# Second layer of the first MLP by seven products: plain products ahead of the sums, long-lived activations in a tile of their own

## The chip, the cores and the metric

One core of a Trainium2 chip runs the whole program. The metric is the device time of one execution in microseconds (us). The kernel before took 576.33 us, the median of 3 runs (575.95 to 576.69).

## The reference, cut to what matters

```python
attn = _attn_ref(q, k, v, lam)                     # blockwise linear attention with decay, 2 x 8 x 768 x 64
x = attn.transpose(0, 2, 1, 3).reshape(1536, 512)
h = np.maximum(x @ moe_w_in, 0.0)                  # 512 -> 2048
x = (h * h @ moe_w_out)                            # 2048 -> 512
h = x @ moe2_w_in                                  # the second MLP: 512 -> 2048 -> 512
out = np.maximum(0.01 * h, h) @ moe2_w_out
```

All inputs of the MLPs but x are 64-bit floats; the output is float32.

## The kernel before, in words

Retention runs first. Then come two MLPs over 1536 tokens, held as three token tiles of 512 (t = 0, 1, 2). The 2048 hidden features are cut into four slices of 512, so each MLP has four stages, named (layer, slice): (0,0) to (0,3) and (1,0) to (1,3). In a stage, `first` computes hidden features (four groups m = 0 to 3 of 128 features for each token tile) and `second` multiplies the activated features by the slice of the second weight and adds the result to a partial sum in DRAM (`spill`).

Every float32 value is kept as a high and a low part (`split`: ScalarE copies the high part, VectorE subtracts to get the low part). A product of two matrices is three matmuls: high by high, high by low, low by high. Each matmul here has 512 columns. The weights arrive as 64-bit words and are converted on VectorE and ScalarE (`converting`), in steps laced between the matmul groups.

The change lies in stages (0,1) and (0,2), the set `seven`. There the second layer for token tiles 0 and 1 is done by `second_pair` with seven block products in place of eight (a Winograd scheme). Its operands are the weight blocks A11 to A22, sums of weight blocks S1 to S4, the activation blocks B11 (token tile 0, even m), B21 (tile 0, odd m), B22 (tile 1, odd m), and sums of activations T1 to T4. `four_sums` (lines 430 to 435) forms T1 to T4 in place in the activations r that `activate_for_seven` keeps in the dictionary `later`. T1 is split at once into the blocks of `g[1]` that no other block uses. T2 is split at once into a tile `tt[2]` of 8 KB per partition. T3 and T4 are split later (`late_split`) into the place of T1 and B21, once these have been read for the last time.

A product is computed for p = 0 and p = 1, six matmuls each. Its result stands in a PSUM bank named by `where`: "A", "B", "C", "D", one for each p. `keep` copies the bank to a buffer f on ScalarE, and a DMA adds f to DRAM. Some products are accumulated on a bank that holds an earlier one, by `start=False`: A12 B21 on A11 B11 (bank A), S4 B22 on S1 T1 (bank C), S3 T3 on S2 T2 (bank B). So bank A is copied once when it holds P1 = A11 B11, and again when it holds the sum.

What sets the order: TensorE's instructions stand in the order in which the code is written (a manual schedule for that engine). On ScalarE and VectorE a scheduler orders them at build time by priority; `tc.high_priority(offset=400)` moves the sums and splits ahead. All engines run their instructions in that order, and the waits between engines follow from the data: a matmul that adds to a bank waits for the copy that reads it. The buffers f come from a pool of nine (`fp`), which `plain()` hands out for activations and copies alike.

Of the kernel before, what the change touches and what calls it, by code (L numbers as in the profile page):

```python
# [9 lines left out]
F32 = mybir.dt.float32  # L10
F32R = mybir.dt.float32r
# [4 lines left out]
P = 128  # L16
# [3 lines left out]
def tile_retention_then_two_mlps(  # L20
# [19 lines left out]
    TT = 512  # L40
# [17 lines left out]
    def bank():  # L58
        return psum.tile([P, 512], F32, tag="ps", name="ps")

    def plain():
        return fp.tile([P, TT], F32, tag="f", name="f")

    def dma(dst, src):
        return nc.sync.dma_start(dst, src)

    def split(hi, lo, src):
        nc.scalar.copy(hi, src)
        nc.vector.tensor_tensor(out=lo, in0=src, in1=hi, op=ALU.subtract)
# [333 lines left out]
    late = ctx.enter_context(tc.tile_pool(name="late", bufs=1, reuse_waits="tile"))  # L403
# [3 lines left out]
    g, x0f, x1f, tt = {}, {}, {}, {}  # L407
# [22 lines left out]
    def four_sums(a, b, c, d):  # L430
        ve = nc.vector
        ve.tensor_tensor(out=a, in0=b, in1=a, op=ALU.subtract)
        ve.tensor_tensor(out=b, in0=c, in1=b, op=ALU.subtract)
        ve.tensor_tensor(out=c, in0=c, in1=a, op=ALU.subtract)
        ve.tensor_tensor(out=d, in0=d, in1=c, op=ALU.subtract)
# [24 lines left out]
    later = {}  # L460


    def activate_for_seven(t, m, src):
        r = plain()
        later[t, m] = r
        nc.scalar.activation(r, src, AF.Relu)
        ghi, glo = g[t]
        if (t, m % 2) != (1, 0):
            nc.scalar.square(ghi[:, m], r)
        nc.scalar.square(r, r)  # L470
        if (t, m % 2) != (1, 0):
            nc.vector.tensor_tensor(out=glo[:, m], in0=r, in1=ghi[:, m], op=ALU.subtract)
        if (t, m % 2) == (1, 1):
            h = m // 2
            with tc.high_priority(offset=400):
                four_sums(later[0, m - 1], later[1, m - 1], later[1, m], later[0, m])
                split(ghi[:, m - 1], glo[:, m - 1], later[0, m - 1])
                if h == 0:
                    tt[2] = late.tile([P, 2, 2, TT], F32R, tag="t4", name="t4")
                split(tt[2][:, 0, h], tt[2][:, 1, h], later[1, m])  # L480

    def three(ps, ops, start, stop, again=False):
        for n, (a, b) in enumerate(ops):
            nc.tensor.matmul(ps, a, b, start=start and n == 0, stop=stop and n == len(ops) - 1, skip_group_check=again)  # L484
# [103 lines left out]
    def keep(src, dst, first):  # L588
        f = plain()
        nc.scalar.copy(f, src)  # L590
        if first:
            dma(dst, f)
        else:
            nc.gpsimd.dma_start(dst, f, accum_op=ALU.add)  # L594
# [3 lines left out]
    def second_pair(s):  # L598
        begun = (0, s - 1) in seven
        (g0h, g0l), (g1h, g1l) = g[0], g[1]  # L600
        x = {
            "B11": [(g0h[:, 2 * h], g0l[:, 2 * h]) for h in range(2)],
            "B21": [(g0h[:, 2 * h + 1], g0l[:, 2 * h + 1]) for h in range(2)],
            "B22": [(g1h[:, 2 * h + 1], g1l[:, 2 * h + 1]) for h in range(2)],
            "T1": [(g1h[:, 2 * h], g1l[:, 2 * h]) for h in range(2)],
            "T2": [(tt[2][:, 0, h], tt[2][:, 1, h]) for h in range(2)],
        }
        ps = {}

        def product(p, where, a, b, start=True):  # L610
            if start:
                ps[p, where] = bank()
            ops = []
            for h in range(2):
                if a[0] == "A":
                    i, j = int(a[1]) - 1, int(a[2]) - 1
                    hi, lo = (w[:, j, (2 * p + i) * P:(2 * p + i + 1) * P] for w in wts[0, s, 1, h])
                else:
                    hi, lo = (sums[0, s, 1, h][:, part, int(a[1]) - 1, p] for part in range(2))
                bh, bl = x[b][h]  # L620
                ops += [(hi, bh), (hi, bl), (lo, bh)]
            three(ps[p, where], ops, start, True, not start)
            return ps[p, where]

        def kept(p, i, k):
            return spill[0][k][2 * p + i]

        def late_split(n, old, m):
            x[n] = x[old]
            with tc.high_priority(offset=400):  # L630
                for h in range(2):
                    split(*x[n][h], later[m(h)])

        both = range(2)
        for p in both:
            keep(product(p, "A", "A11", "B11"), partial[p]["P1"], not begun)
            yield True
        for p in both:
            keep(product(p, "C", "S1", "T1"), kept(p, 1, 1), False)
            yield True  # L640
        late_split("T3", "T1", lambda h: (1, 2 * h))
        for p in both:
            keep(product(p, "A", "A12", "B21", False), kept(p, 0, 0), False)
            yield True
        late_split("T4", "B21", lambda h: (0, 2 * h + 1))
        for p in both:
            keep(product(p, "C", "S4", "B22", False), kept(p, 0, 1), False)
            yield True
        for p in both:
            keep(product(p, "B", "S2", "T2"), partial[p]["P6"], not begun)  # L650
            yield True
        for p in both:
            keep(product(p, "D", "A22", "T4"), kept(p, 1, 0), False)
            yield True
        yield from first(0, s, 2)
        for p in both:
            keep(product(p, "B", "S3", "T3", False), partial[p]["P67"], not begun)
            yield True
        opened.add(("sums", 0, s + 1))
        if (0, s + 1) not in seven:  # L660
            for p in both:
                p1, p6, p67 = (partial[p][n] for n in ("P1", "P6", "P67"))
                for dst, src in ((p67, p1), (kept(p, 0, 1), p1), (kept(p, 0, 1), p6), (kept(p, 1, 0), p67),
                                 (kept(p, 1, 1), p67)):
                    nc.gpsimd.dma_start(dst, src, accum_op=ALU.add, max_dma_last_dim=TT)
# [97 lines left out]
```

## Time and profile before

| | us |
|---|---|
| median of 3 runs | 576.33 |
| the profiled execution, its own time | 577.08 |
| its span, first to last instruction | 575.3 |
| TensorE matmuls busy | 564.5 (98% of the span) |
| VectorE busy | 418.8 (73%) |
| ScalarE busy | 305.4 (53%) |

Matmuls overlap, so that a matmul of 0.39 us is followed by the next one 0.227 us after its start; a busy share of TensorE says only that a matmul was under way. Where TensorE waits in the MLPs is told by the list of its waits, and by the gaps in its timeline. The mean granted clock of TensorE in this execution is 0.999 of full speed.

### The profile page before, as it was taken

To read this page: it belongs to the slowest core of one execution; us is meant where nothing else is said; L and a number is where in the kernel's file an instruction comes from. 1 tells how busy PE (TensorE), PEld (TensorE's weight loads), DVE (VectorE), ACT (ScalarE), POOL (GpSimd) and SP (SyncE) were. 2 spreads that over 40 slices of the span, in tenths; PEclk is the share of its full clock that TensorE was granted. 3 is DMA by queue.
4 is the path that set the end of the run, shared out by engine and by line. 5 is a ranking of instruction groups with operands and counts; after the bars stand their busy time and mean duration, and the time that the engine had idled before them with its cause. 6 is when DMAs were issued, how large, how long until landed. Compare 5 with 4: busy or idle time off the path is not lost.

```text
span 575.3 us, 8057 instructions
## 1 busy us (share of the span) xinstructions
PE 564.5 (98%) x3075; PEld 470.5 (82%) x3075; DVE 418.8 (73%) x589; ACT 305.4 (53%) x477; POOL 84.6 (15%) x101
## 2 busy tenths in 40 slices
PE   7999999999999999999999999999999999999997
PEld 6879888888888887888888888888888888888886
DVE  3789999978618999488789999929873896217222
ACT  2344598547757587756648374543562375225110
POOL 3426000000030205346000000000203011210000
PEclk9999999999999999999999999999999999999999
DMA  8998433663193729999903216452539523661432
GB/s 174 248 203 187 157 117 129 244 197 144 40 181 113 143 74 185 188 226 181 296 25 96 77 46 220 127 166 74 97 59 247 109 27 48 74 91 56 163 111 91
DMA packets 74070, 78.12 MB, mean 136 GB/s; under 512 B 40104, under 2 KB 46512, under 8 KB 74032
## 3 DMA queue, kind: packets, MB, share of 16 engines
q1 hardware_dynamic: 60448, 60.57, 34.6%
q0 software_dynamic: 13056, 16.78, 21.0%
q8 instruction: 24, 0.39, 0.3%
q10 hardware_dynamic: 528, 0.26, 0.2%
q14 instruction: 14, 0.11, 0.1%
HBM read 52.43 MB, written 27.80 MB: 139 GB/s over the span
## 4 chain that ended last, share of the span: by engine, by line
PE 86%; DVE 7%; DMA 4%; issue 2%; ACT 1%; SPq 0%; ACTq 0%; DVEq 0%
PE ps L484 80%; DMA raw<-in_moe_w_in 3%; PE ps L296 1%; PE ps L347 1%; PE ps L279 1%; PE ps L345 1%; DMA DTr<-tab 1%; PE ps L320 1%; ACT hb L109 1%; DVE hb L113 1%; DVE rb L117 1%; DVE Pm L301 1%; DVE hb L110 0%; DVE rb L116 0%; DVE hb L120 0%
## 5 line engine op out<-in xcount | busy, mean ns | idle before, releaser
L484 PE MATMUL ps<-xhi,w1h 128*128 128x512 f32 x288 | 112.3, 390 | 0.0
L484 PE MATMUL ps<-xlo,w1h 128*128 128x512 f32 x288 | 112.2, 389 | 0.0
L484 PE MATMUL ps<-xhi,w1l 128*128 128x512 f32 x288 | 112.1, 389 | 0.0
L594 POOL DMA_DIRECT2D spill<-f x48 | 47.1, 1045 | 345.3 <-ACT f L590 345.2
L590 ACT COPY f<-ps 128x512 f32<-128x512 f32 x84 | 48.9, 585 | 74.1 <-PE ps L484 72.8
L484 PEld LDWEIGHTS ps<-xhi,w1h 128*128 128x128 f32 x288 | 54.1, 188 | 11.4 <-issue 0.2
L484 PEld LDWEIGHTS ps<-xhi,w1l 128*128 128x128 f32 x288 | 54.1, 188 | 11.2
L484 PEld LDWEIGHTS ps<-xlo,w1h 128*128 128x128 f32 x288 | 54.1, 188 | 11.2
L458 DVE TENSOR_TENSOR g0l<-f,g0h 128x512 fp32r<-128x512 f32 x52 | 35.1, 688 | 31.5 <-ACT f L454 20.0
L484 PE MATMUL ps<-w2l,g0h 128*128 128x512 f32 (+1 forms) x132 | 50.5, 383 | 0.0
L484 PE MATMUL ps<-w2h,g0l 128*128 128x512 f32 (+1 forms) x132 | 50.5, 383 | 0.0
L484 PE MATMUL ps<-w2h,g0h 128*128 128x512 f32 (+1 forms) x132 | 50.5, 383 | 0.0
L132 DVE TENSOR_TENSOR w2l<-hb,w2h 128x1024 fp32r<-128x1024 f32 x16 | 19.6, 1225 | 39.5 <-ACT w2h L130 39.2
L109 ACT ACTIVATE hb<-raw 128x1024 f32<-128x1024 f32 x32 | 36.9, 1152 | 20.2 <-DMA raw<-in_moe_w_in 9.3
L484 PE MATMUL ps<-g0l,w2h 128*128 128x512 f32 x104 | 40.5, 390 | 0.0
L484 PE MATMUL ps<-g0h,w2l 128*128 128x512 f32 x104 | 40.5, 389 | 0.0
L484 PE MATMUL ps<-g0h,w2h 128*128 128x512 f32 x104 | 40.5, 389 | 0.0
L117 DVE SCALAR_TENSOR_TENSOR rb<-raw,rb 128x1024 f32<-128x1024 uint32 x32 | 39.1, 1222 | 0.5
L120 DVE TENSOR_TENSOR hb<-hb,rb 128x1024 f32<-128x1024 f32 x32 | 39.1, 1222 | 0.4
L113 DVE SCALAR_TENSOR_TENSOR hb<-raw,hb 128x1024 uint32<-128x1024 uint32 x32 | 39.1, 1221 | 0.3
L548 DVE TENSOR_TENSOR f<-ps,f 128x512 f32<-128x512 f32 x40 | 26.3, 687 | 9.9 <-PE ps L484 9.9
L695 DVE TENSOR_TENSOR f<-ps,f 128x512 f32<-128x512 f32 (+1 forms) x25 | 16.7, 668 | 20.2 <-PE ps L484 20.2
(140 smaller groups left out, 1141.3 us busy)
## 6 DMA issues: line engine op xcount, KB each, us to landing
raw<-in_moe_w_in SPq DMA_DIRECT2D x16, 1024.0 KB, 5.6
raw<-in_moe_w_out SPq DMA_DIRECT2D x16, 1024.0 KB, 4.9
spill<-f POOLq DMA_DIRECT2D x48, 256.0 KB, 4.9
spill<-f SPq DMA_DIRECT2D x24, 256.0 KB, 2.5
f<-spill SPq DMA_DIRECT2D x24, 256.0 KB, 3.0
k<-in_k SPq DMA_DIRECT2D x12, 256.0 KB, 4.6
q<-in_q SPq DMA_DIRECT2D x12, 256.0 KB, 4.8
v<-in_v SPq DMA_DIRECT2D x12, 256.0 KB, 5.1
```

The costliest lines, as they stand in the source:

```text
L109: nc.scalar.activation(hf, w_hi.bitcast(F32), AF.Abs)
L113: yield ve.scalar_tensor_tensor(out=hb, in0=w_hi, scalar=0xC0000000, in1=hb, op0=ALU.bitwise_and, op1=ALU.bitwise_or)
L117: yield ve.scalar_tensor_tensor(out=rf, in0=w_lo, scalar=2.0 ** -52, in1=rf, op0=ALU.mult, op1=ALU.mult)
L120: yield ve.tensor_tensor(out=hf, in0=hf, in1=rf, op=ALU.add)
L132: yield ve.tensor_tensor(out=lo, in0=hf, in1=hi, op=ALU.subtract)
L279: nc.tensor.transpose(ps[:, p, :], src[:, 2 * p:2 * p + 2, :].rearrange("s h d -> s (h d)"), ident)
L458: nc.vector.tensor_tensor(out=glo, in0=r, in1=ghi, op=ALU.subtract)
L484: nc.tensor.matmul(ps, a, b, start=start and n == 0, stop=stop and n == len(ops) - 1, skip_group_check=again)
L548: ve.tensor_tensor(out=out, in0=ps[h, where], in1=other, op=ALU.add)
L590: nc.scalar.copy(f, src)
L594: nc.gpsimd.dma_start(dst, f, accum_op=ALU.add)
L695: nc.vector.tensor_tensor(out=a, in0=ps, in1=a, op=ALU.add)
```

## The change

Three edits, all for the stages (0,1) and (0,2).

1. Four of the eight activations of a stage, (t, m) = (0,1), (0,3), (1,0), (1,2), go into a tile `long` (tag "t4", 8 KB per partition, the place that `tt[2]` had) and no longer into buffers of the pool `fp`.
2. T2 has no tile of its own: it is split late, into the blocks of B11, after A11 B11 has been computed.
3. `second_pair` computes A12 B21 second and S1 T1 third. Before, it was the other way round. The splits of T2, T4 and T3 now stand behind A11 B11, A12 B21 and S1 T1.

```diff
     def activate_for_seven(t, m, src):
-        r = plain()
+        if (t, m) == (0, 0):
+            later["long"] = late.tile([P, 4, TT], F32, tag="t4", name="long")
+        r = plain() if m % 2 == t else later["long"][:, 2 * t + m // 2]
         later[t, m] = r
...
                 split(ghi[:, m - 1], glo[:, m - 1], later[0, m - 1])
-                if h == 0:
-                    tt[2] = late.tile([P, 2, 2, TT], F32R, tag="t4", name="t4")
-                split(tt[2][:, 0, h], tt[2][:, 1, h], later[1, m])
...
-            "T2": [(tt[2][:, 0, h], tt[2][:, 1, h]) for h in range(2)],
...
         for p in both:
             keep(product(p, "A", "A11", "B11"), partial[p]["P1"], not begun)
             yield True
+        late_split("T2", "B11", lambda h: (1, 2 * h + 1))
+        for p in both:
+            keep(product(p, "A", "A12", "B21", False), kept(p, 0, 0), False)
+            yield True
+        late_split("T4", "B21", lambda h: (0, 2 * h + 1))
         for p in both:
             keep(product(p, "C", "S1", "T1"), kept(p, 1, 1), False)
             yield True
         late_split("T3", "T1", lambda h: (1, 2 * h))
-        for p in both:
-            keep(product(p, "A", "A12", "B21", False), kept(p, 0, 0), False)
-            yield True
-        late_split("T4", "B21", lambda h: (0, 2 * h + 1))
         for p in both:
             keep(product(p, "C", "S4", "B22", False), kept(p, 0, 1), False)
             yield True
```

The rows below are TensorE's order in stage (0,2), where `second_pair` begins: the end of A11 B11 for p = 1, and what follows. The number behind `ps` tells the PSUM tiles apart. Before, A11 B11 stands in ps_2267 (p = 0) and ps_2278 (p = 1):

```order
L484 MATMUL ps_2267<-g0h_2069,w2l_2101 128x512
L484 MATMUL ps_2278<-g0h_2069,w2h_1714 128x512
L484 MATMUL ps_2278<-g0l_2070,w2h_1714 128x512
L484 MATMUL ps_2278<-g0h_2069,w2l_1715 128x512
L484 MATMUL ps_2278<-g0h_2069,w2h_2100 128x512
L484 MATMUL ps_2278<-g0l_2070,w2h_2100 128x512
L484 MATMUL ps_2278<-g0h_2069,w2l_2101 128x512
L484 MATMUL ps_2289<-g1h_2119,sw_1994 128x512
```

After, A11 B11 stands in ps_2255 and ps_2266 (line 483 is line 484 of before):

```order
L483 MATMUL ps_2255<-g0h_2065,w2l_2098 128x512
L483 MATMUL ps_2266<-g0h_2065,w2h_1708 128x512
L483 MATMUL ps_2266<-g0l_2066,w2h_1708 128x512
L483 MATMUL ps_2266<-g0h_2065,w2l_1709 128x512
L483 MATMUL ps_2266<-g0h_2065,w2h_2097 128x512
L483 MATMUL ps_2266<-g0l_2066,w2h_2097 128x512
L483 MATMUL ps_2266<-g0h_2065,w2l_2098 128x512
L483 MATMUL ps_2255<-g0h_2065,w2h_1708 128x512
```

Before, a bank of its own (ps_2289) follows on A11 B11, and ps_2267 comes up again twelve matmuls later; after, the matmul that follows adds to ps_2255, six matmuls after the last one that wrote to it.

ScalarE's order at the same place, before; L590 is the copy in `keep`, L466 to L470 are the activations, L68 is a split, L109 begins the conversion of a weight block:

```order
L466 ACTIVATE f_2207<-ps_2193 128x512
L469 ACTIVATE g0h_2069<-f_2207 128x512
L470 ACTIVATE f_2207<-f_2207 128x512
L466 ACTIVATE f_2232<-ps_2215 128x512
L109 ACTIVATE hb_2312<-raw_2212 128x1024
L470 ACTIVATE f_2232<-f_2232 128x512
L466 ACTIVATE f_2253<-ps_2239 128x512
L469 ACTIVATE g1h_2119<-f_2253 128x512
L68 CAST g1h_2119<-f_2187 128x512
L470 ACTIVATE f_2253<-f_2253 128x512
L590 COPY f_2274<-ps_2267 128x512
```

And after (L468, L471, L472 and L589 are L466, L469, L470 and L590 of before):

```order
L109 ACTIVATE hb_2302<-raw_2203 128x1024
L468 ACTIVATE long_2081<-ps_2206 128x512
L472 ACTIVATE long_2081<-long_2081 128x512
L468 ACTIVATE f_2243<-ps_2229 128x512
L471 ACTIVATE g1h_2115<-f_2243 128x512
L68 CAST g1h_2115<-f_2179 128x512
L472 ACTIVATE f_2243<-f_2243 128x512
L68 CAST g0h_2065<-f_2153 128x512
L589 COPY f_2262<-ps_2255 128x512
L589 COPY f_2273<-ps_2266 128x512
L589 COPY f_2287<-ps_2255 128x512
```

The copy of A11 B11 (ps_2255) has a split of T2 ahead of it now, the cast into g0h; the start of a conversion (L109) has moved ahead of the activation of (t, m) = (1,2).

VectorE's order at that place, before; L432, L434 and L435 are in `four_sums`, L132 is the low part of a weight block:

```order
L435 TENSOR_TENSOR f_2110<-f_2110,f_2158 128x512
L69 TENSOR_TENSOR t4_2169<-f_2158,t4_2169 128x512
L132 TENSOR_TENSOR w2l_2223<-hb_2148,w2h_2222 128x1024
L472 TENSOR_TENSOR g0l_2070<-f_2207,g0h_2069 128x512
L116 TENSOR_SCALAR rb_2236<-hb_2235 128x1024
L117 SCALAR_TENSOR_TENSOR rb_2236<-raw_2090,rb_2236 128x1024
L432 TENSOR_TENSOR f_2187<-f_2232,f_2187 128x512
```

And after:

```order
L435 TENSOR_TENSOR long_2081<-long_2081,f_2153 128x512
L132 TENSOR_TENSOR w2l_2214<-hb_2143,w2h_2213 128x1024
L474 TENSOR_TENSOR g0l_2066<-long_2081,g0h_2065 128x512
L116 TENSOR_SCALAR rb_2226<-hb_2225 128x1024
L110 TENSOR_SCALAR hb_2302<-hb_2302 128x1024
L117 SCALAR_TENSOR_TENSOR rb_2226<-raw_2087,rb_2226 128x1024
L432 TENSOR_TENSOR f_2179<-long_2081,f_2179 128x512
```

The low part of T2 (into t4) is gone from this stretch, and a step of a conversion (L110) stands ahead of L432, the first step of T1's second half.

## Rows read from the trace of the kernel before

**Rows 1.** The page, busy time of each engine (us, share of span, instructions).

```profile
PE 564.5 (98%) x3075; PEld 470.5 (82%) x3075; DVE 418.8 (73%) x589; ACT 305.4 (53%) x477; POOL 84.6 (15%) x101
```

**Rows 2.** Waits of TensorE from 60 to 575 us: total, times, longest.

```profile
PE ps L484 <- ACT g1h L68: 0.8, 1, 0.8
PE ps L484 <- DVE g1l L69: 0.6, 1, 0.6
```

**Rows 3.** Timeline of TensorE, stage (0,2): start, duration, instruction, idle before.

```profile
213.31 0.39 PE L484 MATMUL ps<-g0h,w2h 128*128 128x512 f32 x1
...
216.03 0.39 PE L484 MATMUL ps<-g1h,sw 128*128 128x512 f32 x1
...
217.64 0.50 PE L484 MATMUL ps<-g1h,sw 128*128 128x512 f32 x1 [0.77 <-ACT g1h L68]
218.73 0.50 PE L484 MATMUL ps<-g1l,sw 128*128 128x512 f32 x1 [0.58 <-DVE g1l L69]
219.07 0.64 PE L484 MATMUL ps<-g1h,sw 128*128 128x512 f32 x2
```

**Rows 4.** Timeline of ScalarE, stage (0,2).

```profile
210.35 1.06 ACT L130 CAST w2h<-hb 128x1024 fp32r<-128x1024 f32 x1 [1.58 <-DVE hb L120]
211.31 0.61 ACT L68 CAST t<-f 128x512 fp32r<-128x512 f32 x1
211.83 0.59 ACT L466 ACTIVATE f<-ps 128x512 f32<-128x512 f32 x1
...
213.65 0.58 ACT L466 ACTIVATE f<-ps 128x512 f32<-128x512 f32 x1
214.13 1.13 ACT L109 ACTIVATE hb<-raw 128x1024 f32<-128x1024 f32 x1
215.17 0.62 ACT L470 ACTIVATE f<-f 128x512 f32<-128x512 f32 x1
215.69 0.59 ACT L466 ACTIVATE f<-ps 128x512 f32<-128x512 f32 x1
216.31 0.63 ACT L469 ACTIVATE g1h<-f 128x512 fp32r<-128x512 f32 x1
216.97 0.62 ACT L68 CAST g1h<-f 128x512 fp32r<-128x512 f32 x1
...
218.03 1.05 ACT L590 COPY f<-ps 128x512 f32<-128x512 f32 x2
```

**Rows 5.** Timeline of VectorE, stage (0,2).

```profile
212.03 0.69 DVE L69 TENSOR_TENSOR t<-f,t 128x512 fp32r<-128x512 f32 x1
212.63 1.23 DVE L132 TENSOR_TENSOR w2l<-hb,w2h 128x1024 fp32r<-128x1024 f32 x1
...
214.39 0.69 DVE L116 TENSOR_SCALAR rb<-hb 128x1024 uint32<-128x1024 uint32 x1
215.11 1.22 DVE L117 SCALAR_TENSOR_TENSOR rb<-raw,rb 128x1024 f32<-128x1024 uint32 x1
216.25 0.68 DVE L432 TENSOR_TENSOR f<-f 128x512 f32<-128x512 f32 x1
216.85 1.22 DVE L120 TENSOR_TENSOR hb<-hb,rb 128x1024 f32<-128x1024 f32 x1
```

**Rows 6.** Chain that ended last, from 192 to 222 us: start, length, what.

```profile
193.56 7.21 DMA raw<-in_moe_w_in
```

**Rows 7.** The page, DMA issues: count, KB each, median us to landing.

```profile
raw<-in_moe_w_in SPq DMA_DIRECT2D x16, 1024.0 KB, 5.6
```

**Rows 8.** Timeline of TensorE, stage (0,1): first matmul of S1 T1.

```profile
153.47 0.39 PE L484 MATMUL ps<-g1h,sw 128*128 128x512 f32 x1
```

**Rows 9.** Timeline of ScalarE, stage (0,1).

```profile
152.25 0.63 ACT L470 ACTIVATE f<-f 128x512 f32<-128x512 f32 x1
152.78 0.57 ACT L590 COPY f<-ps 128x512 f32<-128x512 f32 x1
```

**Rows 10.** Stretches: length, busy us by engine, PEclk, DMA share, GB/s.

```profile
216.00:219.50 3.50, 2.15 (x8) 1.24 (x7) 3.50 (x6) 3.02 (x6) 0.61 (x2) 1.00 0.41 166
```

## The prediction

> **What bounds the kernel now.** I read the busy times first: matmuls are under way in 98% of the span [rows 1]. So a change can gain only where TensorE stands still, and it costs wherever it makes TensorE stand still. The list of TensorE's waits says where that is: from 60 us, where the MLPs begin, to the end it has two waits, for g1h and g1l, the high and low part of T1 [rows 2]. The timeline places both in stage (0,2). A product of six matmuls takes half of the 2.72 us from the start of A11 B11 (213.31) to the start of S1 T1 (216.03), 1.36 us, and one matmul 0.2267 us [rows 3]. The sixth matmul of S1 T1 would start at 216.03 + 5 x 0.2267 = 217.16 and starts at 219.07. Stage (0,2) thus loses 1.91 us; after each wait the next matmul also comes 0.34 us later instead of 0.227, which is 0.11 us of refilling. Stage (0,1) has no such wait. 1.91 us is all that can be gained here.
>
> Then I read why T1 is late. ScalarE and VectorE lag behind TensorE at that place: the activation of (0,3) starts at 211.83 and those of tile 1 at 213.65 and 215.69, because a weight conversion held ScalarE idle for 1.58 us before 210.35 [rows 4]. VectorE reaches L432, the first step of T1's second half, at 216.25 [rows 5], and the cast that the matmul waits for starts at 216.97, behind it [rows 4].
>
> **The change part by part.** The matmuls stay as many as they were, the DMAs too (the queues of SyncE and GpSimd hold as many, and GpSimd's first four stores of a stage only change their targets). T2's four splits in the two stages are moved, not removed.
>
> *T1.* S1 T1 starts one pair of products (2.72 us) later. In stage (0,2) its second half was needed from 216.03 + 3 x 0.2267 = 216.71 on, and its low part was there at 218.73; it will now be needed from 219.43. Both waits go, if the second half comes no more than 0.7 us later than before. Gain: 1.91 us, whole.
>
> *A12 B21 directly behind A11 B11.* This adds a wait. It adds to bank A, which `keep` must first have copied. Before, the other pair of products gave the copy 2.72 us more. Now TensorE wants ps_2255 back at 216.03, one product after it was filled, and everything behind that matmul on TensorE waits with it. So the question is when ScalarE makes the first copy. Before, it was at 218.03 [rows 4], 2 us after TensorE would now need it done. For after I follow ScalarE's new order with durations and start-to-start steps of before:
>
> - 210.35, the cast of w2, stays; nothing ahead of it has changed its order. T2's cast behind it is gone, so the activation of (0,3) starts at 211.31 instead of 211.83. Its three instructions take 213.65 - 211.83 = 1.82 us: 213.13.
> - L109 is next now. It needs the buffer that VectorE's L132 reads. L132 takes the place of T2's subtraction at 212.03 and ends 1.23 us later, 213.26 [rows 5]; L109 starts at 213.30. It holds ScalarE for 1.04 us (214.13 to 215.17): 214.34.
> - L468 of (1,2), 0.62 (215.69 to 216.31): 214.96. L472, 0.52 (215.17 to 215.69): 215.48. L468 of (1,3), 0.62: 216.10. L471, 0.66 (216.31 to 216.97): 216.76, and here T1's cast waits for VectorE's L432.
> - VectorE: L132 and the low part behind it take 214.39 - 212.63 = 1.76 us, so L116 starts at 213.79 to 213.85. Behind it stands L110, new at this place, which waits for L109's end (213.30 + 1.13 = 214.43): 214.47. One step of 0.60 (216.25 to 216.85) to 0.72 us (214.39 to 215.11) brings L117 to 215.07 to 215.19, and 1.14 us more L432 to 216.21 to 216.33. It ends 0.68 us later [rows 5]. The time that T2's subtraction frees is used up by L110.
> - So T1's cast starts at 216.93 to 217.05, against 216.97 before. It, L472 and T2's cast, which now stands ahead of the copy, take 0.53 us each ((218.03 - 216.97) / 2): the copy of ps_2255 starts at 218.52 to 218.64.
> - The copy takes 0.57 us [rows 9]: done by 219.09 to 219.21. TensorE goes on 0.05 us later (216.97 + 0.62 = 217.59, and the matmul at 217.64).
>
> A12 B21 starts at about 219.2 in place of 216.03, and the refilling adds 0.11: stage (0,2) loses 3.2 to 3.4 us at this place; I take 3.3. T1 is complete by about 218.7 and is needed only at 222: its wait stays away. Nothing hides the loss, as TensorE's order is fixed. The next copy (A11 B11, p = 1) follows 0.53 us later, while TensorE needs it 1.36 us later: no second wait.
>
> In stage (0,1) ScalarE is up with TensorE. The same copy starts at 152.78 there and ends at 153.35 [rows 9]; T2's cast stands behind it in the new order. TensorE can go on at 153.40 and would reach A12 B21 at 153.47 [rows 8]. Margin 0.07 us: cost 0 to 0.1.
>
> *S4 B22 directly behind S1 T1.* The same thing on bank C. For p = 1 ScalarE must first do T3's two casts, the second of which can start only when S1 T1 has ended. The record of the last matmul ends 0.39 us after its start, 0.16 us after the product's last step. Then one cast (0.53), the copy (0.57) and two or three handovers of 0.05: bank C is free 1.36 to 1.41 us after S1 T1's last step, and TensorE wants it after one product, 1.36 us. Where ScalarE has nothing else to do, this is 0 to 0.15 us with the refilling. In stage (0,2) T4's cast stands ahead of the copy of S1 T1 and waits for VectorE, which can add 0.3. The bounds for both stages together are 0 (as before, where a pair of products lay between) and 0.6 us; I take 0.35, near the middle, since the margin is nil.
>
> *The tile `long`.* It takes no time itself. It leaves more buffers f for the copies; no wait of TensorE hung on these [rows 2]: 0. Bounds: nothing to gain, and up to 0.5 us (one copy) where a copy meets its buffer a little later or earlier in the ring; it is nearest to 0.
>
> **Sum**, against the profiled execution's own 577.08 us: -1.91 + 3.3 + 0.05 + 0.35 = +1.79, 578.9 us. That execution is 0.75 us over the median of 576.33, so against the median it is 578.1 us, 0.3% more. Bounds: -1.91 + 3.2 = +1.3 and -1.91 + 3.4 + 0.1 + 0.6 + 0.5 = +2.7, which is 577.6 to 579.0.
>
> **The rivals.**
>
> *Faster: the copy is not late.* The whole chain on ScalarE hangs on the conversion that begins when a weight block lands: that block took 7.21 us [rows 6], where the median is 5.6 [rows 7]. If it, or the conversion after it, comes 1.4 us earlier with respect to TensorE, the copy ends at 217.8, stage (0,2) loses no more than before, and the kernel is even; if it comes 3.2 us earlier, the copy is in time and 1.91 us are gained: 574.4 us. For it speaks that 0.52 us on ScalarE and 0.60 us on VectorE are freed just there. Against it speak the two bounds on T1's cast, 216.76 from ScalarE and 216.9 from VectorE, which both have to move, and that the conversions are laced between activations which follow TensorE. Chance of the full gain 0.13; of something between, within 0.2% of before, 0.2, with 576.3 us.
>
> *T1 stays late as well.* If T1's second half came 0.7 us later than TensorE's new need, both losses would add up. It has more than 3 us in hand once TensorE stands still for bank A, since the same ScalarE serves T1's cast before the copy. Time: 578.1 + 1.9 = 580.0 us; chance 0.02.
>
> *The clock falls.* A standstill of about 3.2 us would be longer than any in these stages, where 1.35 us idle in the 3.5 us from 216.0 left the granted clock at 1.00 [rows 10], the upper of its two levels (2.4 GHz). If the clock fell to 1.2 GHz, each pair of products at the lower level would take 2.72 us more: 578.1 + 2.7 = 580.8 us for one pair. No row shows the clock lower, so I give it 0.05. The Trainium skill (TensorE: Matmul & The Clock Gate, section Why this matters for your kernels) advises against long idle stretches between bursts of matmuls, as the clock then drops to half; by that rule the kernel would come out at 580.8 us or more, and the trace neither bears it out nor excludes it, since its idle stretches are shorter.
>
> **How the numbers follow.** The forecast has 0.60, with its own range of 577.6 to 579.0 us. Even 0.2, full gain 0.13, both late 0.02, clock 0.05. From 575.6 to 579.5 the range holds the forecast and the even case, 0.8 in all. A measurement of this kernel tells 0.2% (1.15 us) from no change. The forecast, at +1.3 to +2.7, lies above that line, and so do T1 late and the clock: slower 0.60 + 0.02 + 0.05 = 0.67; within 0.2%: 0.20; faster: 0.13.
>
> **What would show it.** Right: in stage (0,2) one long wait of the first A12 B21 matmul for the copy in `keep`, some 3 us, with T2's cast directly ahead of that copy on ScalarE; no wait for g1h or g1l; the granted clock still full. Small waits of S4 B22 for the copy of bank C. In stage (0,1) a copy that ends within 0.1 us of TensorE's need. Wrong: A12 B21 without a wait in stage (0,2), or a first copy before 217.8.

## The result, and the profile after

The changed kernel takes 580.69 us (median of 10 runs, 579.68 to 581.62), the kernel before 576.37 us in the 10 runs beside it: 1.0064 times as long, interval 1.0046 to 1.0081. In a second set of runs it was 580.53 against 577.23 us, 1.0056 (1.0036 to 1.0075). By medians the loss is 4.3 and 3.3 us, by means 3.7 and 3.2 us (three of the ten runs of before took 577.9 to 579.2 us, which weigh in a mean and hardly in a median). The forecast was 1.8 us, 578.1 us, and its range ended at 579.5. Direction, place and the one long wait are as forecast, the size is not.

The page of the kernel after, which answers to [rows 1]; the second row is the granted clock in 40 slices:

```profile
PE 568.0 (98%) x3075; PEld 472.3 (82%) x3075; DVE 417.8 (72%) x589; ACT 305.6 (53%) x477; POOL 84.9 (15%) x101
...
PEclk9899999999999998999999999999999999999999
```

As many matmuls, but TensorE is busy 3.5 us longer; 1.1 us of this lies ahead of the MLPs, 1.5 us in stage (0,2). In the clock's row the 8 in the second slice lies ahead of the MLPs; the 8 in the sixteenth slice is new. The waits of TensorE from 60 to 580 us:

```profile
PE ps L483 <- ACT f L589: 3.4, 1, 3.4
```

T1's two waits of [rows 2] are gone, and one for the copy in `keep` has taken their place. TensorE's timeline of the kernel after, stage (0,1) and then stage (0,2) (start, duration, instruction, idle before):

```profile
153.07 0.43 PE L483 MATMUL ps<-g0h,w2h 128*128 128x512 f32 x1
153.34 0.40 PE L483 MATMUL ps<-g0l,w2h 128*128 128x512 f32 x1
...
213.13 0.39 PE L483 MATMUL ps<-g0h,w2h 128*128 128x512 f32 x1
...
215.63 0.39 PE L483 MATMUL ps<-g0h,w2l 128*128 128x512 f32 x1
219.45 0.53 PE L483 MATMUL ps<-g0h,w2h 128*128 128x512 f32 x1 [3.44 <-ACT f L589]
219.79 0.62 PE L483 MATMUL ps<-g0l,w2h 128*128 128x512 f32 x1
220.20 0.63 PE L483 MATMUL ps<-g0h,w2l 128*128 128x512 f32 x1
220.63 0.63 PE L483 MATMUL ps<-g0h,w2h 128*128 128x512 f32 x1
...
223.67 0.40 PE L483 MATMUL ps<-g0h,w2l 128*128 128x512 f32 x1
223.91 0.39 PE L483 MATMUL ps<-g1h,sw 128*128 128x512 f32 x1
```

The first A12 B21 matmul should start at 215.63 + 0.227 = 215.86 and starts at 219.45: 3.59 us of standstill. Behind it the second matmul comes 0.34 us after the first, and the next eight 0.41 to 0.43 us apart, in place of 0.227. The eleven steps from 219.45 to 223.67 take 4.22 us instead of 2.49: another 1.73 us. The stretches show why (length, busy us by engine, PEclk, DMA share, GB/s), beside [rows 10]:

```profile
216.00:219.40 3.40, 0.02 (x1) 0.00 (x0) 3.40 (x5) 3.17 (x7) 0.00 (x0) 1.00 0.48 124
219.40:224.00 4.60, 4.55 (x13) 3.62 (x14) 4.31 (x7) 1.68 (x4) 2.66 (x3) 0.63 1.02 217
```

Full clock during the standstill, a mean of 0.63 behind it: most of that stretch ran at 1.2 GHz. ScalarE in the kernel after, against [rows 4, 9]:

```profile
152.38 0.57 ACT L589 COPY f<-ps 128x512 f32<-128x512 f32 x1
...
210.66 1.05 ACT L130 CAST w2h<-hb 128x1024 fp32r<-128x1024 f32 x1 [1.58 <-DVE hb L120]
211.62 0.59 ACT L468 ACTIVATE long<-ps 128x512 f32<-128x512 f32 x1
...
213.60 1.16 ACT L109 ACTIVATE hb<-raw 128x1024 f32<-128x1024 f32 x1
...
216.43 0.63 ACT L471 ACTIVATE g1h<-f 128x512 fp32r<-128x512 f32 x1
217.26 0.62 ACT L68 CAST g1h<-f 128x512 fp32r<-128x512 f32 x1 [0.20 <-DVE f L432]
217.78 0.62 ACT L472 ACTIVATE f<-f 128x512 f32<-128x512 f32 x1
218.32 0.60 ACT L68 CAST g0h<-f 128x512 fp32r<-128x512 f32 x1
218.82 1.07 ACT L589 COPY f<-ps 128x512 f32<-128x512 f32 x2
```

From w2's cast to T1's cast it is 6.60 us (forecast 6.58 to 6.70), to the copy 8.16 us (forecast 8.17 to 8.29), with T2's cast (g0h) straight ahead of the copy. The cast of w2 itself, however, comes 2.47 us ahead of A11 B11 and not 2.96 as before: the raw block took 7.70 us here, against [rows 6]. The chain of the kernel after:

```profile
193.37 7.70 DMA raw<-in_moe_w_in
```

### The profile page after: what moved, and what is told of

Same layout as the page of the kernel before. It is cut to its first block, busy times and chain, and to the rows that moved or that the text cites. A ratio compares the mean times of both kernels' runs of the same rounds, so it can differ in the third digit from the quotient of the medians.

```text
span 579.4 us, 8049 instructions
## 1 busy us (share of the span) xinstructions
PE 568.0 (98%) x3075; PEld 472.3 (82%) x3075; DVE 417.8 (72%) x589; ACT 305.6 (53%) x477; POOL 84.9 (15%) x101
## 4 chain that ended last, share of the span: by engine, by line
PE 70%; DVE 12%; DMA 9%; issue 3%; ACT 3%; POOL 2%; SPq 0%; DVEq 0%; ACTq 0%; POOLq 0%
PE ps L483 62%; DMA raw<-in_moe_w_in 3%; DMA spill<-f 2%; PE ps L279 2%; PE ps L296 2%; DMA partial0P<-partial0P 2%; PE ps L347 1%; DVE f L694 1%; DMA spill<-partial1P 1%; PE ps L345 1%; DVE rb L117 1%; DMA partial0P<-f 1%; DVE hb L113 1%; ACT hb L109 1%; PE ps L320 1%
## 5 line engine op out<-in xcount | busy, mean ns | idle before, releaser
L589 ACT COPY f<-ps 128x512 f32<-128x512 f32 x84 | 49.1, 585 | 76.2 <-PE ps L483 76.1
L109 ACT ACTIVATE hb<-raw 128x1024 f32<-128x1024 f32 x32 | 36.9, 1152 | 21.1 <-DMA raw<-in_moe_w_in 10.0
L132 DVE TENSOR_TENSOR w2l<-hb,w2h 128x1024 fp32r<-128x1024 f32 x16 | 19.6, 1222 | 39.4 <-ACT w2h L130 39.1
```

What stands on the lines that cost most here:

```text
L109: nc.scalar.activation(hf, w_hi.bitcast(F32), AF.Abs)
L132: yield ve.tensor_tensor(out=lo, in0=hf, in1=hi, op=ALU.subtract)
```

## The experiments

Each loss named below is read between starts of matmuls: 72 matmuls, 16.32 us at 0.2267 us each, lie between A11 B11 of stage (0,2) and the next first layer, and what a kernel takes longer for this stretch is its loss there. It was 18.29 us before (loss 1.97) and 21.87 after (loss 5.55).

**e1_old_order.** The kernel after, with S1 T1 second again; T2's late split and the tile `long` stay.

```diff
         late_split("T2", "B11", lambda h: (1, 2 * h + 1))
+        for p in both:
+            keep(product(p, "C", "S1", "T1"), kept(p, 1, 1), False)
+            yield True
+        late_split("T3", "T1", lambda h: (1, 2 * h))
         for p in both:
             keep(product(p, "A", "A12", "B21", False), kept(p, 0, 0), False)
...
-        for p in both:
-            keep(product(p, "C", "S1", "T1"), kept(p, 1, 1), False)
-            yield True
-        late_split("T3", "T1", lambda h: (1, 2 * h))
```

> The changed kernel with the old order of products (S1 T1 second, A12 B21 third); T2 is still split late into B11's place and the tile long stays. Theory W (the loss is TensorE's wait for the copy of bank A, and the clock that falls behind it): a pair of products lies between A11 B11 and A12 B21 again, so no wait for the copy, the clock stays at full speed, and T1 is late as it was: 576.4 us, within 1 us of the kernel before. Rival L (the late split of T2 and the tile long cost the time, by crowding ScalarE behind A11 B11): 579 to 581 us, like the changed kernel.

577.35 against 576.92 us, ratio 1.0005 (0.9989 to 1.0021). The waits of TensorE in e1:

```profile
PE ps L483 <- DVE g1l L69: 0.6, 1, 0.6
PE ps L483 <- ACT g1h L68: 0.4, 1, 0.4
PE ps L483 <- DVE g0l L458: 0.4, 1, 0.4
```

T1's waits are back, bank A's is gone, and so is the loss. T2's late split and `long` cost nothing that these runs can tell (0.2% at most, by the interval). The third row is in stage (0,3), which comes up again below.

**e2_order_alone.** The kernel before, with only those two products exchanged (the same lines the other way round).

> The kernel before with nothing but the new order of products (A12 B21 with T4's split second, S1 T1 with T3's split third); T2 keeps its tile and is split early, no tile long. Theory W: TensorE waits for the copy of bank A here too, about 0.5 us less than in the changed kernel because no cast of T2 stands ahead of the copy, so a standstill of 2.7 to 3.1 us. If the clock falls behind it as well, 580 us; if the standstill is then too short for that, 577.5 to 578.3 us. Rival L: 576.4 us or less, as T2's split is where it was.

579.02 against 576.92 us, 1.0033 (1.0014 to 1.0052). The order alone makes the kernel slower. In its profile the clock stays at 1.00 through stage (0,2). Its timeline of TensorE:

```profile
218.87 0.50 PE L484 MATMUL ps<-g0h,w2h 128*128 128x512 f32 x1 [2.56 <-ACT f L590]
...
315.17 0.50 PE L484 MATMUL ps<-g0l,w2h 128*128 128x512 f32 x1 [0.92 <-DVE g0l L458]
```

The second row is a wait that no step of the prediction had: in stage (0,3), for VectorE. From start to start the standstill is 2.72 us, as expected, but the time is above the 577.5 to 578.3 us that were expected for a full clock; in the profile stage (0,3) loses 1.43 us.

**e3_copy_first.** The copies of A11 B11 are moved up on ScalarE.

```diff
-            keep(product(p, "A", "A11", "B11"), partial[p]["P1"], not begun)
+            product(p, "A", "A11", "B11")
+            with tc.high_priority(offset=800):
+                keep(ps[p, "A"], partial[p]["P1"], not begun)
```

> The changed kernel with the copies of A11 B11 at a higher priority than the splits: on ScalarE the copy of the first bank then stands directly behind T1's cast, two instructions (1.06 us) earlier. Theory W: the standstill at A12 B21 shrinks by 1.06 us to about 2.5 us; time 1.1 us under the changed kernel, and up to 2.7 us under it if the clock no longer falls. A new wait for bank C is possible, as T4's cast still waits for VectorE: up to 0.5 us. Rival L (the splits and the tile long are the cost): no change against the changed kernel.

579.03 against 577.23 us, 1.0033 (1.0021 to 1.0046). With the copy two places earlier on ScalarE (T2's cast and L472 now stand behind it) the wait shrinks, but does not go away; how much the two places are worth is worked out below, beside the profiles of the unedited kernels. TensorE in e3:

```profile
216.80 0.50 PE L483 MATMUL ps<-g0h,w2h 128*128 128x512 f32 x1 [0.74 <-ACT f L589]
...
224.74 0.50 PE L483 MATMUL ps<-g1h,sw 128*128 128x512 f32 x1 [0.38 <-ACT f L589]
```

**e4_filled.** Twelve matmuls of no use stand where TensorE stood still in stage (0,2).

```diff
+        if s == 2:
+            filler = bank()
+            hi = wts[0, s, 1, 0][0][:, 0, 0:P]
+            for _ in range(12):
+                nc.tensor.matmul(filler, hi, x["B21"][0][0], start=True, stop=True)
         late_split("T2", "B11", lambda h: (1, 2 * h + 1))
```

> The changed kernel with twelve more matmuls in stage (0,2) between A11 B11 and A12 B21: they multiply blocks that are there already into a bank that nobody reads (work that is not part of the computation). They take 12 x 0.2267 = 2.72 us of TensorE, which otherwise stands still there for 3.4 us. Theory W: the standstill shrinks to about 0.7 us, the start of A12 B21 stays where it was (about 6.3 us after the start of A11 B11), and the clock does not fall: about 1.6 us faster than the changed kernel, 579.0 us, no stretch with 0.43 us between matmuls. Rival C (the clock falls for another reason, at that time in the program): 580.7 us, with matmuls 0.43 us apart at the same place; if the extra matmuls simply add to the work, 583.4 us.

579.57 against 576.92 us, 1.0042 (1.0022 to 1.0062); the bank waits are 0.32 and 0.25 us. The clock of the stretch that holds the products behind the fillers:

```profile
216.00:224.00 8.00, 7.68 (x34) 6.06 (x33) 8.00 (x13) 5.50 (x11) 2.66 (x3) 1.00 0.81 181
```

With 2.72 us more of work the kernel is 2.65 us over before, while the change alone was 3.3 and 4.3: filling the standstill cost nothing, and in this profile the clock stayed full. The latter alone proves little, as it stayed full in two of the three profiles of after as well (below).

**e5_own_bank.** A12 B21 gets a bank of its own; P1 is added in DRAM.

```diff
-            keep(product(p, "A", "A12", "B21", False), kept(p, 0, 0), False)
+            keep(product(p, "E", "A12", "B21"), kept(p, 0, 0), False)
...
-                for dst, src in ((p67, p1), (kept(p, 0, 1), p1), (kept(p, 0, 1), p6), (kept(p, 1, 0), p67),
+                for dst, src in ((kept(p, 0, 0), p1), (p67, p1), (kept(p, 0, 1), p1), (kept(p, 0, 1), p6), (kept(p, 1, 0), p67),
```

> The changed kernel with A12 B21 in a bank of its own instead of on top of A11 B11; the sum is then made in DRAM, by adding the P1 that is stored over both stages to the spill block (0,0) once at the end of stage (0,2), two more DMAs of 256 KB from DRAM to DRAM. Theory W: no wait for the copy of bank A, T1 comes in time because S1 T1 stands third, and the clock stays full: the 1.9 us that the kernel before loses at T1 are gained, 574.5 us. Rival L: 579 to 581 us. Rival T (T1 is late by more than the 2.7 us that the order gives it): a wait for g1h or g1l remains, 575 to 576.4 us.

579.09 against 576.92 us, 1.0036 (1.0017 to 1.0055). The time is that of rival L, but not for its reason, and none of the three expected it: the wait went to the next product that adds to a used bank, S4 B22 on bank C. ScalarE in e5, the copy of S1 T1 behind two casts that wait for VectorE:

```profile
221.78 0.62 ACT L68 CAST g0h<-f 128x512 fp32r<-128x512 f32 x1 [0.61 <-DVE f L434]
222.98 0.62 ACT L68 CAST g0h<-long 128x512 fp32r<-128x512 f32 x1 [0.58 <-DVE long L435]
223.51 0.58 ACT L589 COPY f<-ps 128x512 f32<-128x512 f32 x1
```

TensorE then waits 1.96 us, and the clock of e5 falls behind it:

```profile
220.00:224.10 4.10, 2.18 (x10) 1.49 (x8) 4.10 (x7) 2.90 (x7) 3.05 (x4) 1.00 1.05 175
224.10:228.50 4.40, 4.36 (x12) 3.46 (x13) 4.33 (x7) 2.10 (x4) 1.03 (x2) 0.61 0.81 138
```

**e6_own_banks.** As e5, and S4 B22 too gets a bank of its own; S1 T1 is then stored to two spilled blocks.

```diff
+        return f
...
-            keep(product(p, "C", "S1", "T1"), kept(p, 1, 1), False)
+            f = keep(product(p, "C", "S1", "T1"), kept(p, 1, 1), False)
+            nc.gpsimd.dma_start(kept(p, 0, 1), f, accum_op=ALU.add)
...
-            keep(product(p, "C", "S4", "B22", False), kept(p, 0, 1), False)
+            keep(product(p, "F", "S4", "B22"), kept(p, 0, 1), False)
```

> As e5, and S4 B22 has a bank of its own too, so that no product is added to a bank that was filled directly before; S1 T1 goes to both spill blocks by a second DMA (four more DMAs of 256 KB in all, and two from DRAM to DRAM). Theory W, with what e5 showed (the wait went from bank A to bank C): no wait of TensorE longer than 0.3 us in stage (0,2), clock full, 1.9 us less than the kernel before: ratio 0.997, some 574.5 us on the scale of the first runs. Rival S (ScalarE is too late for whatever comes third, in any banks): a wait of 1 us or more turns up at S2 T2 or A22 T4 and the ratio is 1.00 or more.

587.42 against 577.23 us, 1.0185 (1.0163 to 1.0207). The stretch of stage (0,2) took its bare 16.32 us: without the two banks in common the order has no loss there, as theory W had it. That gain was lost behind it, with 10 us more, which neither theory had: the profile has 6.6 us of waits there and a half clock behind the longest. e6 also has six DMAs more than after, so these 10 us are not the price of the order; what made them up was not tested. TensorE's waits in e6:

```profile
PE ps L483 <- DVE g0l L458: 3.3, 3, 1.3
PE ps L483 <- DVE g1l L458: 2.3, 1, 2.3
PE ps L483 <- ACT g1h L453: 1.0, 1, 1.0
```

**e7_first_between.** Old order, and half of the first layer of tile 2 moved in between A11 B11 and S1 T1 (with tile 2's activations in sw0 and sw1).

```diff
-                new_g(t, (l, s) == (0, 0))
+                new_g(t, l == 0 and s < 3)
...
+        yield from first(0, s, 2, range(2))
...
-        yield from first(0, s, 2)
+        yield from first(0, s, 2, range(2, 4))
```

> The old order of products with T2 split late and the tile long, and two of the four groups of token tile 2 (24 matmuls, 5.4 us, which need no sum) moved between A11 B11 and S1 T1; the features of tile 2 then go into two other tiles of the same size. Banks A and C are each filled and added to with other work between. Theory W: T1 has 5.4 us more, no wait for T1, for a bank, or of the clock in stage (0,2): ratio 0.997, some 574.5 us on the scale of the first runs. Rival S: the activations of these two groups load ScalarE just where it trails, so T1's late splits or S1 T1 wait again: ratio 1.00 or more.

583.80 against 577.23 us, 1.0100 (1.0069 to 1.0131). Waits for bank C (1.5 us in all) come behind the moved layer, and stage (0,3) waits 3.3 us for g0l, with matmuls 0.43 us apart behind the last two of its four stops.

**after_again, after_third, before_look, before_look2.** Both kernels unedited, for the spread from one execution to the next.

> The changed kernel once more, unchanged, so that the others of this call have it on their own chip. Theory W (TensorE waits for the copy of bank A in stage (0,2), and the clock falls behind that standstill): 3.4 to 3.6 us of standstill again, and 8 to 9 matmuls at 0.43 us behind it; 3 to 4.5 us slower than the kernel before. Rival C (the clock fell by chance in the first profile): the same standstill and no slow matmuls, 1.7 to 2 us slower.

> The changed kernel, unedited, a third profile. Theory (the wait for bank A is there in every execution, 2.0 to 3.5 us by where ScalarE happens to be; the clock's fall behind it and the waits of stage (0,3) come in some executions): a wait for the copy of 2.0 to 3.6 us; a half clock behind it or not; if it is not there, up to 2 us of waits for g0l in stage (0,3). Rival (the clock's fall is the rule and explains the median): half clock for 6 to 10 matmuls behind the wait, 1.3 to 1.8 us.

> The kernel before, unedited, a second profile, for the waits of stage (0,3). Theory A (these waits follow from the loss in stage (0,2)): T1's two waits in stage (0,2), none for g0l in stage (0,3). Theory B (they come and go in the kernel before too, since VectorE and the DMA chain leave hardly any margin there): in some of the profiles 0.3 to 2 us of waits for g0l at about 310 to 320 us, in the kernel before as well.

> The kernel before, unedited, a third profile. The same as for the second: theory A, no wait for g0l in stage (0,3); theory B, 0.3 to 2 us of it in this or the second profile.

The profiled executions took 581.85 and 577.53 us (after), 576.59 and 576.07 us (before). TensorE in after_again; the clock was 1.00 all through both stages:

```profile
219.32 0.50 PE L483 MATMUL ps<-g0h,w2h 128*128 128x512 f32 x1 [2.05 <-ACT f L589]
...
314.55 0.50 PE L483 MATMUL ps<-g0l,w2h 128*128 128x512 f32 x1 [0.59 <-DVE g0l L458]
...
316.89 0.50 PE L483 MATMUL ps<-g0l,w2h 128*128 128x512 f32 x1 [1.24 <-DVE g0l L458]
```

TensorE and ScalarE in after_third, with neither a low clock nor a wait in stage (0,3):

```profile
213.54 0.39 PE L483 MATMUL ps<-g0h,w2h 128*128 128x512 f32 x1
...
218.10 0.50 PE L483 MATMUL ps<-g0h,w2h 128*128 128x512 f32 x1 [1.69 <-ACT f L589]
```

```profile
209.31 1.05 ACT L130 CAST w2h<-hb 128x1024 fp32r<-128x1024 f32 x1 [1.58 <-DVE hb L120]
...
217.48 1.06 ACT L589 COPY f<-ps 128x512 f32<-128x512 f32 x2
```

Laid beside each other: how long the load of the weight block took, how far w2's cast is ahead of A11 B11 (the lead), and the loss of the stretch:

| profile | load | lead | loss in stage (0,2) |
|---|---|---|---|
| before, as in [rows 3, 4, 6] | 7.21 us | 2.96 us | 1.97 us |
| before_look | 6.47 us | 3.72 us | 1.17 us |
| before_look2 | 6.02 us | 4.16 us | 0.76 us |
| after | 7.70 us | 2.47 us | 5.55 us (1.73 of it the slow steps) |
| after_again | 6.32 us | 3.87 us | 2.53 us |
| after_third | 5.95 us | 4.23 us | 2.18 us |

In all six the load starts 19.75 to 19.78 us ahead of A11 B11, and load and lead together are 10.17 to 10.19 us: the lead differs only by how long the load took. The copy starts 8.16 to 8.17 us behind the cast in all three profiles of after, and the wait is 5.91 to 5.92 us less the lead (3.44 + 2.47; 2.05 + 3.87; 1.69 + 4.23). Other runs in this order bear that out. x2 (lead 3.76 us) should wait 2.16 us and waits 2.14. e2 (2.85 us), which has no cast of T2 ahead of the copy, waits 0.51 us less than the 3.07 of after. e3 (4.13 us), with the copy two places earlier, waits 1.05 us less than 1.79; 1.06 was expected. e4 (2.87 us) waits 0.32 us where after would wait 3.05: its 2.72 us of fillers stand in the difference.

Both kernels lose about a microsecond less for each that the weight block is earlier, so at the same lead they stay some 1.5 us apart. No profile of before has a wait for g0l in stage (0,3), so that theory B of before_look found nothing to bear it out.

**e8_new_in_first.** The kernel before, with the new order in stage (0,1) alone.

```diff
...
+        for part in (a12b21, s1t1) if s == 1 else (s1t1, a12b21):
+            yield from part()
```

Here `a12b21` and `s1t1` hold the lines of the two products with the late split behind each.

> The kernel before, with the new order of products (A11 B11, A12 B21, S1 T1, S4 B22) in stage (0,1) alone; stage (0,2) keeps the order of before, T2 and the buffers are as before. Theory (the loss is the wait for bank A in stage (0,2), where ScalarE is behind TensorE; the order itself costs nothing where ScalarE is up with it): within 0.2% of before, at most +0.2 us in stage (0,1), T1's two waits of stage (0,2) as in the kernel before (together 0.9 to 1.9 us), no other new wait of TensorE ahead of stage (0,3). Rival (the new order costs in every stage, by the waits for banks A and C and their refilling): 1 us or more lost in stage (0,1), 578 us or more.

577.31 against 576.65 us, 1.0011 (0.9996 to 1.0025). Stage (0,1) lost 0.24 us, just over the 0.2 expected (62.80 us in place of 62.56 from its A11 B11 to that of stage (0,2)). T1's waits cost 0.52 us in its profile, less than expected; its lead, 4.38 us, is the longest of all. Where ScalarE is up with TensorE the order is nearly free.

**x1_before_no_adds, x2_after_no_adds, x3_filled_no_adds.** Before, after and e4 without the ten DRAM additions behind stage (0,2); their output lacks that part of the first MLP.

```diff
-                for dst, src in ((p67, p1), (kept(p, 0, 1), p1), (kept(p, 0, 1), p6), (kept(p, 1, 0), p67),
-                                 (kept(p, 1, 1), p67)):
+                for dst, src in ():
```

> The kernel before, without the ten transfers behind stage (0,2) that add the partial products P1, P6 and P67 to the spilled sums in DRAM; that part of the first MLP's second layer is so left out of the output. It is the base line for the next two kernels. Both theories: T1's two waits in stage (0,2), no wait for g0l in stage (0,3); 0 to 1 us less than before, since these waits were seen in none of the profiles of before.

> The changed kernel, without the same ten transfers (the same part left out). Theory A (what is lost over the wait for bank A comes from stage (0,3), where the loads of spilled sums stand behind these additions and VectorE then hands g0l over late): no wait for g0l in stage (0,3), and against the base line without the additions 1.3 to 2.2 us more, in place of the 3.3 to 4.3 us that the change costs with them. Theory B (the half clock behind the wait for bank A is the bulk of the rest): 3.3 us or more over the base line all the same, and a granted clock that falls behind the wait.

> The changed kernel without the ten transfers, with twelve matmuls of 512 columns of no use between A11 B11 and A12 B21 of stage (0,2), which keep TensorE at work where it would stand still. Worked out from these: 12 x 0.2267 = 2.72 us of extra work, up to 0.6 us of waits for banks A and C, less the 0.8 to 1.9 us that T1's waits take in the base line: 1.4 to 2.5 us over the base line. Theory A: within 1 us of the changed kernel without fillers. Theory B: at least 1 us faster than that kernel although it does twelve matmuls more, as the clock stays up.

577.45, 579.94 and 579.45 us (576.78 for before; 1.0009, 1.0049 and 1.0039, each within 0.002). By medians the change costs 2.5 us without the additions, 3.3 and 4.3 with them. That is between the two theories, over A's 2.2 and under B's 3.3, and each of these figures is good to 1 us or more by the intervals, so that they do not tell the two apart. x1, expected to be 0 to 1 us faster than before, was 0.7 us slower, which its interval allows. In the profile of x2 stage (0,2) loses 1.52 us more than in x1 and stage (0,1) 0.24 more, 1.76 us together; neither a low clock nor a wait for g0l shows in its list, though stage (0,3) loses 0.29 us in stops too short for it:

```profile
PE ps L483 <- ACT f L589: 2.1, 1, 2.1
```

x3 does 2.72 us more work than x2, takes 0.43 us longer in stage (0,2), and still has a median 0.5 us lower. That points to about 0.9 us that the standstill costs beyond itself on average, as by clock falls in some executions; with intervals of 0.2% it is a hint. By the letter theory A is met (x3 within 1 us of x2) and theory B is not (x3 1 us faster). In x3 one wait of 0.2 us for g0l came without the additions, so they are not the only thing that makes that wait.

## Why the prediction was wrong

The step that failed is the end of the sum: behind the waits for banks A and C it had no term. It put the clock's fall behind the standstill at nothing (a rival with 0.05), and what stage (0,3) makes of a late weight block was not in it at all. The runs showed both, each in some executions: 1.73 us of slow matmuls in the first profile of after, and up to 2.63 us lost in stage (0,3).

**Right: the wait, its cause and its place.** The only wait in the list of after is the forecast one; T1's are gone. e1 and e2 show that the order of products alone makes it, e3 and the three profiles of after that it is the copy's place behind T1's and T2's casts, and e5 and e6 that it comes of the bank in common. The steps on ScalarE came out within 0.1 us, counted from w2's cast. e8 confirms that stage (0,1) costs little. S4 B22's waits took 0.10 and 0.16 us, 0.26 of the 0.35 allowed. `long` at zero stands with e1.

**Right only as a difference: the sum of stage (0,2).** Its two terms were both taken from one execution, in which the weight block was late. With an earlier block T1's waits cost 0.5 to 1.2 us (before_look, before_look2, e8) rather than 1.91, and bank A's 2.0 to 2.4 with the refilling (after_third, after_again, x2) rather than 3.3. At the lead of [rows 4], 2.96 us, the relation above gives a wait of 2.96 us, which is 3.2 from start to start (0.15 more) with the refilling (0.11), so the forecast of 3.3 was not luck. At equal lead the gap between the kernels is 1.5 us in stage (0,2) and 0.2 in stage (0,1): 1.7, close to the +1.79 of the sum; T1 and bank A follow the same weight block, so that the difference holds where neither term does. For the same reason the rival of an early block was reckoned wrongly: after_third had it 1.27 us earlier and was no nearer to an equally early execution of before, which gains as well.

**Wrong: "the granted clock still full", chance 0.05.** In after's profiled execution the fall made the steps behind the standstill 1.73 us longer (0.11 of it refilling), of 4.12 us that it lies above the profiled execution of before. The price set for a fall (2.7 us for a pair) was too high, since the clock came back within that pair, but the chance was far too small. [Rows 10] had only shown that shorter standstills, broken by matmuls, left the clock alone; that says nothing of 3.4 us on end. In after_again and after_third, with 2.05 and 1.69 us of idle, the clock stayed at 1.00: the fall is no part of every execution. The Trainium skill (TensorE: Matmul & The Clock Gate, section Why this matters for your kernels) advises against long idle stretches between bursts of matmuls, as the clock then drops to half. After's profile agrees with it, at 0.63 behind 3.44 us of idle; the prediction had cited it, and then outweighed it by rows that could not speak against it.

**Missing: stage (0,3).** The sum ended with the bank waits. Stage (0,3) has hardly any room on VectorE: between its first addition of a spilled block and the last g0l lie 26.96 to 26.99 us in before, before_look, after, after_again and after_third (27.9 in before_look2, where the addition comes earliest), so what delays the former delays the latter. And the addition follows a weight block once more: its load starts 24.4 to 24.5 us ahead of TensorE's second layer in stage (0,3), ScalarE's L109 waits for it to land, and VectorE's L110 for L109. ScalarE and VectorE in before:

```profile
261.03 1.12 ACT L109 ACTIVATE hb<-raw 128x1024 f32<-128x1024 f32 x1 [2.40 <-DMA raw<-in_moe_w_in]
```

```profile
262.19 0.69 DVE L110 TENSOR_SCALAR hb<-hb 128x1024 f32<-128x1024 f32 x1 [2.10 <-ACT hb L109]
```

And in after_again, where the first addition also waits for the load of the spilled block:

```profile
264.59 1.12 ACT L109 ACTIVATE hb<-raw 128x1024 f32<-128x1024 f32 x1 [4.17 <-DMA raw<-in_moe_w_in]
```

```profile
265.74 0.69 DVE L110 TENSOR_SCALAR hb<-hb 128x1024 f32<-128x1024 f32 x1 [3.86 <-ACT hb L109]
...
289.16 0.69 DVE L694 TENSOR_TENSOR f<-ps,f 128x512 f32<-128x512 f32 x1 [1.26 <-DMA f<-spill]
...
316.15 0.69 DVE L458 TENSOR_TENSOR g0l<-f,g0h 128x512 fp32r<-128x512 f32 x1
```

The load of the weight block, the first addition counted from the start of the second layer, and what TensorE loses over the 192 matmuls from there on (43.52 us without a stop):

| profile | load | first addition | loss in stage (0,3) |
|---|---|---|---|
| before_look2 | 6.63 us | 5.45 us | 0 |
| before | 7.58 us | 6.38 us | 0 |
| after_third | 7.62 us | 6.38 us | 0 |
| before_look | 8.14 us | 6.99 us | 0 |
| after | 8.46 us | 7.31 us | 0.25 us |
| x2 (no additions) | 8.58 us | 7.32 us | 0.29 us |
| e1 | 8.81 us | 7.72 us | 0.66 us |
| e2 | 9.63 us | 8.46 us | 1.43 us |
| after_again | 9.50 us | 9.69 us (1.26 of it the spilled block) | 2.63 us |

The time of the addition is that of the load less 1.1 to 1.3 us, the wait for the spilled block left out, and past some 7.05 us the loss grows microsecond for microsecond. Before_look was 0.06 us from it, and e1, in the old order, is past it: the loss does not need the new order, only a slow load. e5, e6 and e7 wait there too; in e6 and e7 the addition comes at 17.0 and 13.2 us, far later than the load explains. After_third, e3 and e4 do not wait. In x1 and x2 the load took 8.22 and 8.58 us without the ten additions, which speaks against these as the cause of a slow load.

**What stays open.** Of the 3.3 to 4.3 us, 1.7 us are shown, in every profile of after, as the exchange of waits. The rest, 1.6 to 2.6 us of the medians, goes with the clock's fall and with stage (0,3), which the profiles show in some executions and not in others; that the two make up the whole rest is not shown. Between the three profiles of each kernel the mean gap is 3.6 us: 0.2 in stage (0,1), 2.1 in (0,2) with 0.5 of it the slow steps of one profile, 1.0 in (0,3) nearly all from after_again, 0.2 in (1,0), and 0.1 ahead of the MLPs, a part which alone takes 94.0 to 95.7 us by execution. x1 to x3 are too coarse to divide the rest. What makes the same load take 6.6 us in one execution and 9.5 in the next, and whether the change makes it slower (6.6 to 8.1 us in three profiles of before, 7.6 to 9.5 in three of after), was not found.

## What to carry to other kernels

When products that need nothing late are moved forward, ask what else they need: an accumulation onto a bank just filled needs its copy, and moves that copy onto the path. Price both orders with the same execution and move the late input for both; a wait that depends on when a transfer lands has a spread, and its gain has the same spread. A long standstill is priced both with a half clock behind it and without: that one standstill left the clock up (2.56 us in e2) does not say that a shorter one will (1.96 us in e5). And look one stage on for an engine without room: here VectorE passed on the delay of a weight block as a wait of TensorE some 50 us later.

## What the runs showed of the hardware

The fall of the clock does not follow from the length of the wait alone. It fell behind 3.44 us (after), behind 1.96 us (e5), and did not behind 2.56 us (e2), 2.05 us (after_again) or 2.14 us (x2). In e6 and e7 it fell where stops came close together (0.99 and 2.29 us in e6; 0.90, 0.71, 1.67 and 0.69 us in e7, where its mean was 0.52 over the 5 us behind the third). In after, once down, it came back within the pair of products: from 223.19, the tenth matmul, the steps are 0.25 us and less. In e6 it stood at 0.50 behind the wait of 2.29 us, for 13 steps of 0.42 us and more:

```profile
294.40:300.00 5.60, 5.60 (x13) 4.44 (x14) 3.54 (x6) 1.86 (x3) 0.00 (x0) 0.50 0.64 231
```

A matmul that restarts TensorE is followed 0.34 us later by the next, and not 0.227: 0.11 us per stop, in all these kernels at full clock.

The load of one weight block of 1024 KB took from 5.79 us (e8) to 7.70 us (after) at the place of stage (0,2), and from 6.37 us (e4) to 9.63 us (e2) at that of stage (0,3), in programs that start it at the same distance from TensorE's work.
